# Dividing two query blocks at once, with new ranks and spans in a kernel that schedules itself

## The chip, the cores and the metric

One core of a Trainium2 chip. The metric is the device time of one execution in microseconds (us); most executions agree within 0.3%. A ratio compares with runs of the kernel before on the same chip, in the same rounds. It is the mean time of one kernel's runs over the mean of the other's, so it is not quite the ratio of the medians that stand beside it. The brackets are 95% intervals.

## The reference, cut to what matters

Four layers over a sequence of 2048 rows of 512: attention, FFN, attention, FFN, each on a normalised input and added to the residual. Both attention layers share weights, and so do both FFN layers.

```python
def _A_ref(x, wqkv, wo):                      # 32 heads of 16, window of 256
    ...
    scores = jnp.einsum("bhqd,bhkd->bhqk", q, k) * (Dh ** -0.5)
    mask = (idx[:, None] - idx[None, :] >= 0) & (idx[:, None] - idx[None, :] < W)
    p = _softmax(jnp.where(mask[None, None], scores, -1e9), axis=-1)
    o = jnp.einsum("bhqk,bhkd->bhqd", p, v)
    ...
x = x + _A_ref(_layernorm(x), A_wqkv, A_wo)
x = x + _B_ref(_layernorm(x), B_w1, B_w2)     # 512 -> 1792, relu, -> 512
x = x + _A_ref(_layernorm(x), A_wqkv, A_wo)
x = x + _B_ref(_layernorm(x), B_w1, B_w2)
```

## The kernel before

The sequence is cut into chunks of 512 rows: two attention-and-FFN layers make eight steps k = 0 to 7. The kernel does not issue instructions as its code reads. It first makes a list of operations (each with its possible engines, an assumed duration on each, what it waits for, and a key). Then it plays them through in Python against these assumed durations, and issues each operation when it is chosen there. So the chip gets one fixed order for each engine, and an engine never takes a later instruction because an earlier one still waits. The smallest key goes first on TensorE; the other engines add the key to the time at which an operation became ready.

```python
SOON = {"qkv": 0, "v": 0, "h": 0, "mask": 0, "div": -1, "add": -1}      # ranks of the kinds of work
LINK = {"PE": 0.3, "DVE": 0.2, "ACT": 0.2, "POOL": 0.2, "SP": 0.2}      # assumed delay from one engine to another
...
def choose(e, t):
    ...
        key = (o.key, o.number) if e == "PE" else (at + o.key, o.number)
```

Scores and exponentials have the lowest keys, then P·V (the sums `acc`), the output projection, and last the dense work, which fills the rest. Dense work has its place by number of score group: q, k and v of a step 16 groups ahead of their use, the FFN of a step from d0 to d1 after its last score group.

```python
wait = 0 if k == 0 else 16                                # in plan_qkv: how far ahead q, k, v are made
...
d0, d1 = base[k + 1] + 9, base[k + 1] + 28                # in plan_rest: the span of the FFN
...
t = op(-5, {"SP": (1.22, lambda ...: sp.dma_start_transpose(out=to(), in_=O_of[k][:, j, :]...), 2.6)}, ready, ob, [ob])
```

The last number of the transpose, 2.6, is what the schedule counts from its issue to its landing. When the schedule would leave TensorE idle for 0.4 us or more, it puts in a filler, a matmul of the identity that computes nothing ("warm"):

```python
if t - idle_since[0] >= (0.4 if t > 20 else 0.0) and ...:
    ... mm(box.tile([P, 512], FP32, "warm")[:], ident[:], ...)
```

After P·V of a block of 128 queries (8 heads), VectorE divides by the sums, one block at a time:

```python
def divide(t, j, acc, O, chk):
    rinv = chk[:, j, 8 * t:8 * t + 8].rearrange("p (a e) -> p a e", e=2)
    dve.reciprocal(rinv, acc[:, :, :, 16])
    dve.tensor_tensor(out=O[:, j, P * t:P * (t + 1)]..., in0=acc[:, :, :, 0:16], in1=rinv..., op=ALU.mult)
```

## Time and profile before

| | before |
|---|---|
| time, median of the first 3 runs | 484.17 us (483.27 to 485.19) |
| span of the profiled run | 482.5 us |
| PE, DVE, ACT, POOL busy | 96%, 76%, 70%, 65% |
| granted TensorE clock | 1.00 |

The tables are read with the prediction, which shows their lines. In those lines PE is TensorE, PEld its weight loads, DVE VectorE, ACT ScalarE, POOL GpSimd and SP (SPq) the engine that issues the DMAs. The tiles are: Sps the scores, Pb their exponentials, acc P·V and its sums, chk the inverse sums, O the divided output, OT its transpose by DMA, ps_d a result of dense work, hT the FFN's hidden rows, xn and xnT normalised rows and their transposes, KBD and V2f the spread keys and values, x_sb the residual, ob the output. One number is not in any view and is used all through: the **gaps of TensorE**, the distance of each matmul's start from the start of the one before, less the pitch at which such matmuls follow each other when nothing holds them (the prediction gives the pitches; for the last matmul of a score block it is its usual distance to the next instruction). What is left over is time that TensorE lost, 38.0 us in the kernel before. Some traces lack about 70 matmul records of some 5900; their weight loads are recorded, so the missing places are known, and 216 ns are taken off for each. Time lost to a halved clock is in the gaps, since the pitch is that of the full clock.

### The profile page before, as it was taken

The page shows a single profiled execution, that of the slowest core. Times are in us where ns is not written, and L with a number is a line of the kernel's source. Part 1 is how long each engine was busy: PE and PEld are TensorE (multiplying, and loading weights), DVE is VectorE, ACT ScalarE, POOL GpSimd, SP SyncE. Part 2 cuts the span into 40 slices and gives each one's busy share as a digit, 9 for nine tenths or more (in the row PEclk, how much of TensorE's full clock was granted, in tenths as well). Part 3 has the DMA queues.
Part 4 walks back from the last instruction along what each step waited for, and adds up shares of the span by engine and source line. Part 5 has one row for each costly group of instructions (what it writes and reads, how often), then busy time and mean ns, then how long its engine had stood idle before and what let it go on. Part 6 is the DMA issues. An engine that isn't in the chain of part 4 may idle for free.

```text
span 482.5 us, 14414 instructions
## 1 busy us (share of the span) xinstructions
PE 461.9 (96%) x5935; PEld 242.3 (50%) x5935; DVE 366.4 (76%) x960; ACT 337.2 (70%) x268; POOL 312.4 (65%) x708
## 2 busy tenths in 40 slices
PE   7889899998899999999999999999999999999995
PEld 3555556654445545554544554455555545554442
DVE  6989899858897789878989977898758876473101
ACT  3877877877777767876778877777876787735240
POOL 7778878768876778777878767677655566520000
PEclk9999999999999999999999999999999999999999
DMA  8770231004300142002311023020153002000101
GB/s 271 244 206 3 45 45 25 2 3 67 67 1 3 24 67 46 3 1 45 58 34 33 13 35 47 12 46 1 24 89 57 13 1 56 24 14 12 35 12 37
DMA packets 54649, 21.98 MB, mean 46 GB/s; under 512 B 46128, under 2 KB 54064, under 8 KB 54576
## 3 DMA queue, kind: packets, MB, share of 16 engines
q1 hardware_dynamic: 54576, 20.98, 19.8%
q8 instruction: 48, 0.79, 0.7%
q14 instruction: 25, 0.20, 0.2%
HBM read 7.86 MB, written 2.10 MB: 21 GB/s over the span
## 4 chain that ended last, share of the span: by engine, by line
PE 72%; DVE 10%; DMA 7%; POOL 6%; issue 2%; ACT 2%; DVEq 0%; ACTq 0%; POOLq 0%
PE ps_d L106 52%; PE acc L106 12%; PE Sps L106 8%; DMA OT<-O 4%; POOL Pb L106 3%; ACT Pb L106 2%; DVE KBD L106 1%; DVE st L106 1%; DMA xn2T<-xn 1%; DVE xn L106 1%; DVE Pb L106 1%; POOL xn L106 1%; DVE x_sb L106 1%; DVE V2f L106 1%; DMA xnT<-xn 1%
## 5 line engine op out<-in xcount | busy, mean ns | idle before, releaser
L106 ACT ACTIVATE Pb<-Sps 128x2048 bf16<-128x2048 f32 (+4 forms) x160 | 283.3, 1770 | 94.4 <-PE Sps L106 75.8
L106 POOL TENSOR_SCALAR_AFFINE_SELECT Pb<-Pb 64x256 bf16<-64x256 bf16 x518 | 222.9, 430 | 99.3 <-ACT Pb L106 77.4
L106 PE MATMUL ps_d<-xn2T,w 128*128 128x512 bf16 (+1 forms) x504 | 109.5, 356 | 1.2 <-DVE hT L106 0.9
L106 PE MATMUL ps_d<-w,hT 128*128 128x512 bf16 x448 | 109.0, 380 | 0.0
L106 PEld LDWEIGHTS <-Pb 128*128 128x128 bf16 x2880 | 83.5, 96 | 25.6 <-issue 8.6
L106 PE MATMUL acc<-V2f,Pb 128*128 128x34 bf16 x2880 | 90.1, 178 | 2.3 <-POOL Pb L106 1.3
L106 PE MATMUL ps_d<-xnT,wqkv 128*128 128x512 bf16 (+1 forms) x288 | 66.5, 356 | 2.2 <-DMA xnT<-xn 1.0
L106 PEld LDWEIGHTS <-w 128*128 128x128 bf16 x504 | 45.3, 97 | 44.7 <-issue 5.4
L106 PE MATMUL Sps<-Qt,KBD 32*128 32x192 bf16 (+4 forms) x1472 | 61.6, 252 | 2.8 <-ACT Pb L106 2.5
L106 PEld LDWEIGHTS <-hT 128*128 128x128 bf16 x448 | 40.3, 98 | 46.0 <-issue 3.6
L106 DVE TENSOR_TENSOR Pb<-Pb,tri 128x512 bf16<-128x512 bf16 (+1 forms) x136 | 58.8, 437 | 5.0 <-ACT Pb L106 4.6
L106 DVE TENSOR_SCALAR hT<-ps_d 128x512 bf16<-128x512 f32 (+1 forms) x74 | 45.8, 625 | 11.4 <-PE ps_d L106 10.9
L106 PEld LDWEIGHTS <-KBD 32*128 32x128 bf16 x1472 | 24.0, 92 | 51.7 <-issue 48.9
L106 DVE TENSOR_SCALAR KBD<-ps_d,par 128x256 bf16<-128x256 f32 (+1 forms) x82 | 45.5, 604 | 1.6 <-PE ps_d L106 1.5
L106 DVE BATCH_NORM_STATS2 st<-x_sb 128x6 f32<-128x512 f32 (+1 forms) x64 | 43.7, 683 | 0.9 <-DMA x_sb<-in_A_x_dram 0.6
L106 ACT ACTIVATE hT<-ps_d 128x512 bf16<-128x512 f32 (+1 forms) x52 | 28.4, 550 | 20.9 <-PE ps_d L106 19.4
L106 DVE TENSOR_TENSOR x_sb<-ps_d,x_sb 128x512 f32<-128x512 f32 x48 | 32.7, 684 | 13.0 <-PE ps_d L106 12.4
L106 DVE TENSOR_TENSOR O<-acc,chk 128x128 bf16<-128x128 f32 x128 | 37.3, 291 | 4.5 <-DMA OT<-O 0.2
L106 DVE RECIPROCAL chk<-acc 128x8 f32<-128x8 f32 x128 | 25.6, 200 | 17.7 <-PE acc L106 15.2
L106 PEld LDWEIGHTS <-wqkv 128*128 128x128 bf16 x288 | 25.7, 97 | 26.1 <-issue 4.0
L106 DVE TENSOR_TENSOR ob<-ps_d,x_sb 128x512 bf16<-128x512 f32 x16 | 11.0, 690 | 34.4 <-PE ps_d L106 34.3
L106 PE MATMUL ps_d<-wo,OT 128*128 128x512 bf16 x128 | 32.5, 380 | 3.9 <-DMA OT<-O 3.6
(55 smaller groups left out, 300.3 us busy)
## 6 DMA issues: line engine op xcount, KB each, us to landing
w<-in_B_w_dram SPq DMA_DIRECT2D x2, 1792.0 KB, 10.0
out_dram<-ob SPq DMA_DIRECT2D x16, 128.0 KB, 1.7
wqkv<-in_A_wqkv_dram SPq DMA_DIRECT2D x3, 512.0 KB, 7.0
x_sb<-in_A_x_dram SPq DMA_DIRECT2D x3, 512.0 KB, 8.9
x_sb<-in_A_x_dram SPq DMA_DIRECT2D x2, 256.0 KB, 2.9
wo<-in_A_wo_dram SPq DMA_DIRECT2D x1, 512.0 KB, 8.9
xnT<-xn SPq DMA_TRANSPOSE x28, 2.5
OT<-O SPq DMA_TRANSPOSE x28, 2.5
```

The costliest lines, as they stand in the source:

```text
L106: inst = fn(*a, **k)
```

## The change

The intent: halve the number of divisions, which gives VectorE time back, and set the schedule's ranks and spans anew.

```diff
-    SOON = {"qkv": 0, "v": 0, "h": 0, "mask": 0, "div": -1, "add": -1}
-    LINK = {"PE": 0.3, "DVE": 0.2, "ACT": 0.2, "POOL": 0.2, "SP": 0.2}
+    SOON = {'qkv': -0.5, 'v': 0, 'h': -1, 'mask': -1, 'div': 0, 'add': -2}
+    LINK = {"PE": 0.2, "DVE": 0.2, "ACT": 0.2, "POOL": 0.2, "SP": 0.2}
...
     def divide(t, j, acc, O, chk):
-        rinv = chk[:, j, 8 * t:8 * t + 8].rearrange("p (a e) -> p a e", e=2)
-        dve.reciprocal(rinv, acc[:, :, :, 16])
-        dve.tensor_tensor(out=O[:, j, P * t:P * (t + 1)]..., in0=acc[:, :, :, 0:16], ...)
+        sums = acc[:].rearrange("p j a e d -> p j (a e) d")
+        rinv = chk[:, j:j + 2, 8 * t:8 * t + 8]
+        dve.reciprocal(rinv, sums[:, :, :, 16])
+        dve.tensor_tensor(out=O[:, j:j + 2, P * t:P * (t + 1)]..., in0=sums[:, :, :, 0:16], ...)
...
-            for jl in range(u.nq // 2):
+            for j0 in range(0, u.nq // 2, 2):
                 box = Box(psum)
+                prior = None
+                for jl in (j0, j0 + 1):            # two blocks, one after the other, into one accumulator
...
-                            box.ps = box.tile([P, 4, 2, 17], FP32, "acc")
+                                box.ps = box.tile([P, 2, 4, 2, 17], FP32, "acc")
...
-                divs[k, u.t, j] = op(SOON["div"], {"DVE": (0.5, dfn)}, ...)
+                divs[k, u.t, j] = divs[k, u.t, j + 1] = op(SOON["div"], {"DVE": (0.64, dfn)}, ...)
...
-                d0, d1 = base[k + 1] + 9, base[k + 1] + 28
+                d0, d1 = base[k + 1] + 7, base[k + 1] + 24
```

More of the change, by code (lines that the diff above doesn't have):

```diff
@@ L392, in divide @@
     def divide(t, j, acc, O, chk):
-        rinv = chk[:, j, 8 * t:8 * t + 8].rearrange("p (a e) -> p a e", e=2)
-        dve.reciprocal(rinv, acc[:, :, :, 16])
-        dve.tensor_tensor(out=O[:, j, P * t:P * (t + 1)].rearrange("p (a e d) -> p a e d", a=4, e=2),
-                          in0=acc[:, :, :, 0:16],
-                          in1=rinv.rearrange("p a (e o) -> p a e o", o=1).to_broadcast([P, 4, 2, 16]), op=ALU.mult)
+        sums = acc[:].rearrange("p j a e d -> p j (a e) d")
+        rinv = chk[:, j:j + 2, 8 * t:8 * t + 8]
+        dve.reciprocal(rinv, sums[:, :, :, 16])
+        dve.tensor_tensor(out=O[:, j:j + 2, P * t:P * (t + 1)].rearrange("p j (a d) -> p j a d", d=16),
+                          in0=sums[:, :, :, 0:16],
+                          in1=rinv.rearrange("p j (a o) -> p j a o", o=1).to_broadcast([P, 2, 8, 16]), op=ALU.mult)
     def accumulate_check(chk, first):
@@ L558, in plan_attention @@
                     masks[s].append(op(SOON["mask"], options(times, lambda e, m=m, g=g, pb=pb: mask(e, m, places(pb, g))), [exps[s]] + c_tri))
-            for jl in range(u.nq // 2):
-                kbs = seen(u, jl)
-                need = []
-                for g in sorted({u.place[kb][0] for kb in kbs}):
-                    need += [exps[first_slot[n] + g]] + masks[first_slot[n] + g]
-                for kb in kbs:
-                    b = u.q0 + kb
-                    need.append(v_done[k, b // 2] if b >= 0 else v_done[k - 1, (b + 8) // 2])
-                j = u.q0 // 2 + jl
+            for j0 in range(0, u.nq // 2, 2):
@@ L568, in plan_attention @@
                 box = Box(psum)
                 prior = None
-                for p in range(4):
-                    def pfn(u=u, jl=jl, pb=pb, box=box, p=p):
-                        if p == 0:
-                            box.ps = box.tile([P, 4, 2, 17], FP32, "acc")
-                        pv_group(u, jl, p, pb, box.ps)
-                    prior = op(-5e4 + n - (1000 if p else 0), {"PE": (0.025 * len(kbs) + (0.03 if p == 0 else 0.0), pfn)},
-                               [prior] if p else need, None if p else box, [box])
@@ L578, in plan_attention, with pfn @@
-                pvs[n, jl] = prior
+                for jl in (j0, j0 + 1):
+                    kbs = seen(u, jl)
+                    need = [prior]
+                    for g in sorted({u.place[kb][0] for kb in kbs}):
+                        need += [exps[first_slot[n] + g]] + masks[first_slot[n] + g]
+                    for kb in kbs:
+                        b = u.q0 + kb
+                        need.append(v_done[k, b // 2] if b >= 0 else v_done[k - 1, (b + 8) // 2])
+                    for p in range(4):
+                        begins = jl == j0 and p == 0
+                        def pfn(u=u, jl=jl, j0=j0, pb=pb, box=box, p=p, begins=begins):
+                            if begins:
+                                box.ps = box.tile([P, 2, 4, 2, 17], FP32, "acc")
+                            pv_group(u, jl, p, pb, box.ps[:, jl - j0])
+                        prior = op(-5e4 + n - (0 if begins else 1000),
+                                   {"PE": (0.025 * len(kbs) + (0.03 if p == 0 else 0.0), pfn)},
+                                   need if p == 0 else [prior], box if begins else None, [box])
+                    pvs[n, jl] = prior
@@ L580, in dfn @@
+                j = u.q0 // 2 + j0
                 def dfn(u=u, j=j, box=box):
@@ L583, in plan_attention @@
                 war = [turned[k - 1, i] for i in range(4)] if k else []
-                divs[k, u.t, j] = op(SOON["div"], {"DVE": (0.5, dfn)}, [pvs[n, jl]] + war + checks[k - 2:k - 1], None, [box])
+                divs[k, u.t, j] = divs[k, u.t, j + 1] = op(
+                    SOON["div"], {"DVE": (0.64, dfn)}, [prior] + war + checks[k - 2:k - 1], None, [box])
         checks.append(op(40, {"DVE": (1.1, lambda k=k: accumulate_check(chks[k % 2], k == 0))},
```

## The prediction

> **What bounds the kernel now.** I began with the page's busy shares, went on to the groups of instructions by shape (what one matmul costs), then to the chain of work that ended last in order of time (how fast matmuls follow each other), then to busy time by stretch (where TensorE is idle), and last to the waits.
>
> ```profile
> span 482.5 us, 14414 instructions
> PE 461.9 (96%) x5935; PEld 242.3 (50%) x5935; DVE 366.4 (76%) x960; ACT 337.2 (70%) x268; POOL 312.4 (65%) x708
> ```
>
> ```profile
> 180.86 1.05 PE acc L106 x42
> 184.94 2.27 PE ps_d L106 x10
> 443.10 34.33 PE ps_d L106 x159
> 477.45 0.69 DVE ob L106
> ```
>
> The busy share of PE says little by itself, since a matmul's recorded 380 ns overlaps its neighbours. The pitch in the chain is the true cost: 34.33/159 = 216 ns for a matmul of 512 columns, 1.05/42 = 25 ns for one of the small P·V matmuls (34 columns). The trace starts 256-column matmuls 109 ns and transposes 56 ns apart, and a score group, seen from its start to the start of what follows, takes about 0.33 us. Counts from the groups by shape times these pitches: 1320 x 0.216 = 285.1; 176 x 0.109 = 19.2; 2880 x 0.025 = 72.0; 160 x 0.33 = 52.8; 48 transposes x 0.056 = 2.7; 38 fillers ("warm", which compute nothing) x 0.216 = 8.2. The sum is 440.0 us of the span of 482.5 us. All but the fillers is work that no order of instructions removes.
>
> So 42.5 us are left over. About 1.5 are before the first matmul, and 5.1 after the last one (477.4 us: a last addition on VectorE, then the last store). I took the distance of each start on PE from the one before, less the pitch, over the whole trace: 20.6 us lie in 41 gaps longer than 0.15 us, and 17.4 us in many small ones, above all some 60 ns at each of the 160 entries into a score group. Busy time by stretch shows where PE is plainly idle (columns: length, then busy time of PE, PEld, DVE, ACT, POOL):
>
> ```profile
> 20.00:60.00 40.00, 36.44 (x565) 21.48 (x564) 36.64 (x102) 31.44 (x32) 34.28 (x80) 1.00 0.31 80
> 60.00:105.00 45.00, 43.97 (x656) 26.50 (x653) 38.07 (x108) 34.98 (x26) 33.13 (x75) 1.00 0.13 21
> 105.00:140.00 35.00, 31.25 (x430) 15.78 (x429) 29.84 (x81) 26.62 (x19) 28.69 (x67) 1.00 0.28 47
> 140.00:300.00 160.00, 158.14 (x2184) 80.84 (x2184) 135.78 (x342) 120.53 (x79) 121.48 (x277) 1.00 0.18 30
> 300.00:420.00 120.00, 118.68 (x1620) 61.17 (x1621) 91.62 (x235) 91.66 (x66) 75.27 (x171) 1.00 0.17 34
> ```
>
> The reader is to see that PE is idle 3.6 us in 20 to 60 us and 3.7 us in 105 to 140 us, and only 3.2 us in the 280 us from 140 to 420 us. The granted clock is 1.00 throughout. The waits name VectorE, GpSimd and ScalarE often, but most of these are those engines waiting for work while PE is full:
>
> ```profile
> POOL Pb L106 <- ACT Pb L106: 77.4, 77, 3.9
> ACT Pb L106 <- PE Sps L106: 75.8, 114, 1.7
> DVE chk L106 <- PE acc L106: 15.2, 25, 2.0
> PEld L106 <- DMA OT<-O: 6.7, 9, 1.4
> PE ps_d L106 <- DMA OT<-O: 3.6, 5, 1.2
> ```
>
> **What the Trainium skill says.** "TensorE: Matmul & The Clock Gate", section "Back-to-back issue gap", gives 518 cycles at 2.4 GHz for 512 columns (216 ns) and a floor near 25 ns for up to 64 columns; the trace has exactly these pitches. The same section also names about 131 ns for 512 columns as the sustained figure of a real kernel; this trace, with 216 ns over 159 matmuls, does not agree. "Perfetto Trace Analysis", section "Optimizing Scalar/DVE Operations", says that grouping into larger operations helps if the engine is saturated: VectorE is at 76% of the span, but 85% in 105 to 140 us (29.84 of 35) and 92% in 20 to 60 us. "VectorE: DVE Perf Modes", section on the TRN2 errata, gives (N+151)/0.96 ns for an fp32 addition of two tensors; for the multiplication by the inverse sums it fits this trace: 291 ns at N=128, by the formula 290.6. "PSUM — Partial Sum Buffer", section "The four PSUM rules", says that a bank holds 512 fp32 per partition and that a first matmul clears the accumulation bits of its whole bank: two query blocks are 2 x 136 = 272 fp32 and fit, and the new code closes one block's sums before it opens the next, so nothing is lost. No run here has shown that yet.
>
> **The change part by part.**
>
> ```profile
> L106 DVE TENSOR_TENSOR O<-acc,chk 128x128 bf16<-128x128 f32 x128 | 37.3, 291 | 4.5 <-DMA OT<-O 0.2
> L106 DVE RECIPROCAL chk<-acc 128x8 f32<-128x8 f32 x128 | 25.6, 200 | 17.7 <-PE acc L106 15.2
> ```
>
> 1. The paired division. Removed: 128 x (0.291 + 0.200) = 62.8 us of VectorE. Added: 64 multiplications of 256 elements and 64 reciprocals of 16. Estimates: (256+151)/0.96 = 424 ns; 200 + 8 x 1.04 = 208 ns, the slope from 291 ns at 128 and 684 at 512 elements. 64 x 0.632 = 40.4. Saved: 22.4 us.
>
> 2. What the ranks move between engines. In the order of the built programs VectorE takes 16 more copies into V2f (x 370 ns = 5.9), 4 more double masks (x 495 = 2.0), 2 more normalisations (1.1) and 3 more half evictions of h (1.2), and one less of Q (0.4): +9.8. Net VectorE: 366.4 - 22.4 + 9.8 = about 354 us. GpSimd loses 16 selects (x 430 = 6.9), 16 copies (x 420 = 6.7) and 2 normalisations (2.7): 312 - 16 = 296 us. ScalarE: the same to 1 us.
>
> 3. TensorE. Every count of real matmuls is the same; fillers 40 in place of 38: +0.4 us. Work on PE: 440.0 + 0.4. So none of the saving is on the engine that sets the end, and the change can win only from gaps.
>
> 4. FFN spans and the PE link. The last P·V of the last step stands after 389.0 us of PE work in the order before and after 392.2 us in the new one, so about 3 us of dense work have moved from the tail, where PE is full anyway, into the attention stages. That is worth something only where PE had a gap there. A lower assumed delay of 0.2 in place of 0.3 for PE puts dependants closer behind their producers: fewer planned gaps, more real ones.
>
> 5. The gaps, by what ended them in the trace (of the 20.6 us): DMA of OT 4.5; ScalarE's Pb 4.7; VectorE after the start 4.1; GpSimd's masks 1.9; the rest startup, xnT and the K eviction. From VectorE's I expect half back (-2), from masks and exponentials -1 (mask rank -1, additions -2), from the earlier FFN -1.5. OT I expect to get worse: the division of a pair waits for its second block. In the order the first output projection of a pair stands 3.2 to 4.9 us of PE work behind the last P·V it needs (3.2 in step 1, 3.7 to 3.8 in steps 3 to 5), and in the trace before the projections that stopped PE started 4.4 to 8.0 us after theirs (others were ready after 3.6 to 3.9 us). +1. Sum: -2 - 1 - 1.5 + 1 + 0.4 = -3.1, so 484.2 - 3.1 = about 481 us.
>
> **The rivals.** (a) The saved VectorE time buys nothing, because PE is the bound: for it, 158.14 of 160 us busy from 140 to 300 us. It makes 484. (b) The pair becomes a wait: both transposes of O become ready together, the DMA queue takes them 1.2 us apart, and the residual and norm behind them start later. For it, the OT gaps above; against it, in most steps dense work of the next step stands ready. It makes 486 to 488. (c) The ranks fill the starved stretches: 20 to 60 and 105 to 140 us hold 10.5 us of the gaps over 0.15 us and the 16 fillers outside the start 3.5 us. If most of that went, it would make 474. Against it: the new order has 8 fillers at the first place again, and 12 in place of 8 at the second. (d) The accumulators become scarce: from first to last P·V matmul they are held 146 us in all in place of 84. But there are half as many divisions to wait for, and four buffers x 480 us to be had. It makes no change.
>
> **Range and chances.** Mine lies between (a) and (c), a little nearer to (a). The floor of 432 us of useful matmuls plus start, end and entries leaves about 20 us of gaps, and 2% would be half of them. I predict 481 us, 475.5 to 486.5 eight times in ten. Faster by over 2% (under 474.6): 0.07. Within: 0.89. Slower (over 494): 0.04.
>
> **What would show it.** In the profile after: reciprocals of 128x16 near 208 ns and multiplications of 128x256 near 424 ns, 64 of each; VectorE near 354 us; real matmuls at the same pitches; PE idle less in 105 to 140 us; waits of PE and PEld for OT as large as before or larger. If VectorE falls and PE's gaps do not, (a) is right. If the starved stretches vanish and the time is under 475 us, I have sized the ranks too small; if PE waits for OT grow by several us, (b) is right.

## The result, and the profile after

482.47 us median (481.79 to 482.80, 4 runs) against 484.23 us (483.27 to 485.19, 4 runs). The ratio is 0.9962 [0.9939, 0.9985]: a gain of 0.4%, inside the 2% that count as the same. In later rounds, on chip 14 (kernel 5 below), the two kernels could not be told apart.

The page after, first two lines; beside the lines before, VectorE has 104 instructions and 6.7 us less, GpSimd 11.7 us less. (PE lacks 73 of its 5937 records here, as the count beside PEld shows, so its busy time is too small.)

```profile
span 479.9 us, 14186 instructions
PE 454.9 (95%) x5864; PEld 242.1 (50%) x5937; DVE 359.7 (75%) x856; ACT 337.1 (70%) x266; POOL 300.7 (63%) x670
```

The groups by shape of the division after (busy, mean ns of one, idle before):

```profile
L106 DVE TENSOR_TENSOR O<-acc,chk 128x256 bf16<-128x256 f32 x64 | 27.1, 424 | 2.5 <-DVE chk L106 0.3
L106 DVE RECIPROCAL chk<-acc 128x16 f32<-128x16 f32 x64 | 16.1, 252 | 17.1 <-PE acc L106 16.5
```

The division took 37.3 + 25.6 = 62.9 us before and takes 27.1 + 16.1 = 43.2 us now: 19.7 us are saved.

Waits after (total us, times, longest), for the lines shown of before:

```profile
POOL Pb L106 <- ACT Pb L106: 89.0, 86, 4.4
ACT Pb L106 <- PE Sps L106: 73.4, 113, 2.3
DVE chk L106 <- PE acc L106: 16.5, 29, 2.1
PEld L106 <- DMA OT<-O: 9.9, 16, 1.9
PE ps_d L106 <- DMA OT<-O: 3.9, 4, 1.5
```

Waits of TensorE and its weight loads for the transposed O have grown from 6.7 + 3.6 to 9.9 + 3.9 us, in 20 places in place of 14. One of them, in the chain in order of time: the transpose takes 4.19 us from its issue until the output projection can start, where the schedule counts 2.6.

```profile
112.53 0.44 DVE O L106
112.97 0.11 SPq L106
113.07 0.04 issue
113.12 4.19 DMA OT<-O
117.31 0.05 issue
117.35 1.91 PE ps_d L106 x8
```

The gaps of TensorE by stretch, all sizes:

| stretch, us | before | after |
|---|---|---|
| 0 to 20 | 5.1 | 5.4 |
| 20 to 60 | 7.1 | 5.5 |
| 60 to 105 | 3.1 | 2.5 |
| 105 to 140 | 6.2 | 5.1 |
| 140 to 300 | 9.8 | 10.7 |
| 300 to 420 | 6.4 | 5.2 |
| after 420 | 0.1 | 0.0 |
| sum | 38.0 | 34.2 |

So 3.8 us of gaps went, two more fillers cost 0.4, and the last addition on VectorE starts at 474.10 us in the chain after where it started at 477.45 us before: 3.35 us earlier. The last store took some 0.7 us longer in this profile, so the span is 2.6 us shorter; the medians differ by 1.8 us.

### The profile page after: what moved, and what is told of

Same layout as the page of the kernel before. It is cut to its first block, busy times and chain, and to the rows that moved or that the text cites. A ratio compares the mean times of both kernels' runs of the same rounds, so it can differ in the third digit from the quotient of the medians.

```text
span 479.9 us, 14186 instructions
## 1 busy us (share of the span) xinstructions
PE 454.9 (95%) x5864; PEld 242.1 (50%) x5937; DVE 359.7 (75%) x856; ACT 337.1 (70%) x266; POOL 300.7 (63%) x670
## 4 chain that ended last, share of the span: by engine, by line
PE 72%; POOL 8%; DMA 7%; DVE 6%; issue 3%; ACT 2%; POOLq 0%; DVEq 0%; ACTq 0%; SPq 0%
PE ps_d L106 51%; PE acc L106 13%; PE Sps L106 8%; POOL Pb L106 4%; DMA OT<-O 3%; DMA xnT<-xn 3%; ACT Pb L106 2%; POOL xn L106 2%; POOL V2f L106 1%; DVE st L106 1%; POOL rstds L106 1%; DVE V2f L106 1%; DVE KBD L106 1%; DVE xn L106 1%; POOL nbs L106 1%
## 5 line engine op out<-in xcount | busy, mean ns | idle before, releaser
L106 POOL TENSOR_SCALAR_AFFINE_SELECT Pb<-Pb 64x256 bf16<-64x256 bf16 x502 | 219.9, 438 | 109.6 <-ACT Pb L106 89.0
L106 PE MATMUL ps_d<-xn2T,w 128*128 128x512 bf16 (+1 forms) x486 | 106.8, 355 | 2.4 <-issue 0.9
L106 PE MATMUL ps_d<-w,hT 128*128 128x512 bf16 x427 | 103.7, 379 | 1.7 <-issue 1.0
L106 PEld LDWEIGHTS <-Pb 128*128 128x128 bf16 x2880 | 83.5, 96 | 25.6 <-issue 9.3
L106 DVE TENSOR_TENSOR Pb<-Pb,tri 128x512 bf16<-128x512 bf16 (+1 forms) x140 | 61.5, 444 | 16.9 <-ACT Pb L106 16.5
L106 PE MATMUL ps_d<-xnT,wqkv 128*128 128x512 bf16 (+1 forms) x271 | 63.7, 354 | 2.9 <-issue 1.1
L106 PE MATMUL Sps<-Qt,KBD 32*128 32x192 bf16 (+4 forms) x1472 | 61.5, 252 | 1.0 <-ACT Pb L106 0.7
L106 DVE TENSOR_SCALAR hT<-ps_d 128x512 bf16<-128x512 f32 (+1 forms) x77 | 46.6, 617 | 12.4 <-PE ps_d L106 12.3
L106 ACT ACTIVATE hT<-ps_d 128x512 bf16<-128x512 f32 (+1 forms) x49 | 27.5, 561 | 22.4 <-PE ps_d L106 22.0
L106 POOL TENSOR_TENSOR rstds<-rstds,mhalf 128x2 f32<-128x2 f32 (+1 forms) x33 | 23.6, 718 | 14.5 <-DVE rstds L106 12.0
L106 PE MATMUL ps_d<-wqkv,xnT 128*128 128x512 bf16 x118 | 31.4, 379 | 0.6 <-issue 0.2
```

The source lines that it names most:

```text
L106: inst = fn(*a, **k)
```

## The experiments

Twelve kernels ran, four at a time on one chip each, all with five rounds and all with the reference's results. The table gathers them. "Account" is the time that the kernel's own scheduler comes to by its assumed durations; "lost" is fillers x 0.216 us plus the gaps, both of the profiled run.

| kernel | fillers | gaps, us | of these over 0.15 us and ended by OT | lost, us | account, us | median, us | ratio to before |
|---|---|---|---|---|---|---|---|
| before (profile of its first runs) | 38 | 38.0 | 4.5 | 46.2 | 482.2 | 484.2 | |
| changed | 40 | 34.2 | 5.5 | 42.8 | 480.3 | 482.47 | 0.9962 [0.9939, 0.9985] |
| 1 pair alone | 44 | 37.0 | 3.7 | 46.5 | 483.3 | 485.08 | 1.0016 [1.0002, 1.0031] |
| 2 ranks alone | 34 | 42.3 | 6.3 | 49.6 | 484.9 | 486.50 | 1.0033 [1.0019, 1.0048] |
| 3 spans alone | 38 | 38.2 | 3.9 | 46.4 | 483.9 | 484.78 | 1.0007 [0.9994, 1.0020] |
| 4 changed, VectorE padded | 40 | 37.6 | 5.2 | 46.2 | 480.3 | 485.09 | 1.0027 [1.0007, 1.0047] |
| 5 changed, again | 40 | 34.7 | 4.9 | 43.3 | 480.3 | 483.53 | 1.0005 [0.9982, 1.0028] |
| 6 changed, span end 23 | 53 | 35.2 | 5.4 | 46.6 | 483.7 | 485.49 | 1.0046 [1.0019, 1.0072] |
| 7 single, searched | 36 | 35.6 | 3.6 | 43.4 | 478.7 | 481.89 | 0.9972 [0.9948, 0.9995] |
| 8 changed without the pair | 34 | 45.0 | 6.7 | 52.3 | 483.7 | 487.77 | 1.0090 [1.0064, 1.0117] |
| 9 pair, 3.2 us, searched | 34 | 31.1 | 1.0 | 38.5 | 477.3 | 477.60 | 0.9867 [0.9845, 0.9890] |
| 10 single, 3.2 us, searched | 36 | 30.7 | 2.2 | 38.5 | 479.4 | 477.09 | 0.9864 [0.9844, 0.9884] |
| 11 as 9, searched, no fillers | 20 | 34.2 | 1.0 | 38.5 | 477.1 | 479.59 | 0.9910 [0.9894, 0.9926] |
| 12 as 10, searched, no fillers | 20 | 37.8 | 1.0 | 42.1 | 478.8 | 481.02 | 0.9938 [0.9923, 0.9953] |

Kernels 1 to 4 shared 11 runs of before with a median of 484.56 us, 5 to 8 a median of 483.74, 9 to 12 a median of 484.08. Each kernel has 4 to 6 runs. In kernels 11 and 12 one wait of 1.4 us lies between two score blocks that follow each other directly; it is counted here.

Two things in this table are to be kept in mind. First, gaps and lost are those of one run. The profiled runs of kernels 1, 2 and 8 are slower than their medians (486.19, 487.94 and 490.48 us), and in each of them the granted clock is halved for 3.4 us in mid-kernel (6.8 us in kernel 8). By the gaps within these windows that took 1.1, 1.5 and 2.6 us. Second, the account needs no chip. Kernel 5 repeats the changed kernel, and the account doesn't see the padding of kernel 4; for the other eleven, whether the account lies above or below that of the kernel before agrees with whether the median does. The sizes do not: kernel 10 was 2.8 us shorter by the account and 7.0 us on the chip.

**First set: which part made the gain?** I held that the ranks had made it (theory A); the rivals were the freed VectorE time (B) and the FFN spans (C).

Kernel 1, the pair alone:

```diff
 (the paired division of the change)
+    SOON = {"qkv": 0, "v": 0, "h": 0, "mask": 0, "div": -1, "add": -1}     # as before
+    LINK = {"PE": 0.3, ...}                                                # as before
+                d0, d1 = base[k + 1] + 9, base[k + 1] + 28                 # as before
```

> The kernel before with the paired division alone; old ranks, old PE link, old FFN spans. Theory A (the ranks made the gain; the pair only frees VectorE, which is not the bound, and delays the output projections): 484 to 485.5 us, with VectorE some 20 us less busy than before, 44 fillers in the order in place of 38, and larger waits for OT. Rival B (the freed VectorE time made the gain): about 482 us, gaps that VectorE ends gone.

Measured: 485.08 us, ratio 1.0016. VectorE was 353.9 us busy, 12.5 less than before where I expected 20, and the order has 44 fillers. The forecast of A holds for the time, not in its reason: the gaps ended by OT did not grow (3.7 us). The gaps fell by 1.0 us (the profiled run's half-clock window, 1.1 us, included) and the six fillers more cost 1.3. VectorE time was freed here, and what it may have bought went into fillers.

Kernel 2, the ranks and the link alone:

```diff
+    SOON = {'qkv': -0.5, 'v': 0, 'h': -1, 'mask': -1, 'div': 0, 'add': -2}
+    LINK = {"PE": 0.2, ...}
```

> The kernel before with the new ranks and the PE link of 0.2 alone; single divisions, old spans. Theory A: about 482 us or a little below, with fewer gaps between 20 and 60 us and after 300 us; its order has 34 fillers in place of 38. Rival B: 484 us, as before. Rival C (the FFN spans made the gain): 484 us.

Measured: 486.50 us, ratio 1.0033, slower than before. Theory A falls. The order has the fewest fillers of this set but the most gaps, 42.3 us, of which 1.5 lie in a half-clock window. The scheduler's own account, 484.9 us against 482.2, had said slower too.

Kernel 3, the spans alone:

```diff
-                d0, d1 = base[k + 1] + 9, base[k + 1] + 28
+                d0, d1 = base[k + 1] + 7, base[k + 1] + 24
```

> The kernel before with the new FFN spans alone (7 to 24 in place of 9 to 28). The order is the same up to about the 70th score group. Theory A: 484 us within 1 us, because PE is already full after 140 us. Rival C: about 482 us, with the gaps after 300 us gone.

Measured: 484.78 us, ratio 1.0007. C falls too. After 300 us the gaps went from 6.4 to 4.9 us, but between 140 and 300 us they rose from 9.8 to 12.0. The gaps were moved and not removed.

So no part gains by itself: +0.16, +0.33 and +0.07%, and yet all three together gained 0.4% in the first rounds. The parts don't add. (By the account they don't either: 483.3, 484.9 and 483.9 us for the parts, 482.2 for the kernel before, 480.3 for the whole.)

Kernel 4, the changed kernel's own order with VectorE made slower by an instruction that does nothing:

```diff
         dve.tensor_tensor(out=O[:, j:j + 2, ...], in0=sums[:, :, :, 0:16], ...)
+        dve.tensor_tensor(out=tri[:], in0=tri[:], in1=tri[:], op=ALU.min)
```

> The changed kernel with one idle VectorE instruction (a minimum of a constant with itself, some 0.25 to 0.3 us) after each of the 64 paired divisions; order and scheduler's times unchanged. It gives back 16 to 19 us of the 19.7 us of VectorE time that the pairing freed. Theory A: 482.5 to 483.2 us, at most 0.7 us slower than the changed kernel. Rival B: 484 us or more, the gain gone.

The instructions on this tile in the profile of kernel 4 (ns min/median/max, first and last start):

```profile
L106 DVE TENSOR_TENSOR tri<-tri x64: 246/250/470, 22.9 to 429.9; 128x192 bf16<-128x192 bf16 x64
```

Measured: 485.09 us, ratio 1.0027. 64 x 0.25 = 16 us of VectorE time brought the gaps from 34.2 back to 37.6 us, 1.8 us of it between 20 and 60 us. Against the kernel before nothing of the changed kernel's gain is left. The changed kernel did not run in these rounds, though; its ratios elsewhere, 0.9962 and 1.0005 (kernel 5), put the cost of the padding at 0.7% or 0.2%, 1 to 3 us. So in a fixed order VectorE's time does seem to count, by some 2 us for 16: this speaks for B, where kernel 1 speaks against it. The two differ in one thing. In kernel 4 the order stays, and in kernel 1 the scheduler made a new order out of the shorter divisions.

**Second set: is it the order?** A new theory (D): each alteration of a number gives another order, orders differ by some us whatever the reason for the alteration, and the settings of the change are ones that came out well with the pair. The rival (E): pair and ranks belong together, and their gain is robust.

Kernel 5 is the changed kernel, unaltered.

> The changed kernel once more, as the base of this set: 482 to 483 us, 0.4% under the kernel before, if the first result holds on this chip.

Measured: 483.53 us beside 483.74 for the kernel before, ratio 1.0005 [0.9982, 1.0028]. The profile agrees with the first one (gaps 34.7 us, span 480.5), but three of the six runs had a mean granted clock of 0.994 to 0.995 and took 484.0 to 484.3 us; the other three took 482.3 to 483.1. No run of the kernel before had under 0.998 here. The third set comes back to this.

Kernel 6, one number altered by one:

```diff
-                d0, d1 = base[k + 1] + 7, base[k + 1] + 24
+                d0, d1 = base[k + 1] + 7, base[k + 1] + 23
```

> The changed kernel with one number altered by one: the FFN span ends at 23 in place of 24. Pair and ranks stay. Theory D (the gain is that of one particular instruction order out of many; every small alteration of a rank gives another order, and the new settings are a picked one): the scheduler's own account lengthens by 3.4 us and the order has 53 fillers in place of 40, so 484.5 to 487 us, slower than the kernel before. Theory E (the gain belongs to the paired division together with the ranks and is robust): within 1 us of the changed kernel.

Measured: 485.49 us, ratio 1.0046, that is 0.4% over the changed kernel in the same rounds. Busy time of the fillers alone, by stretch, between 140 and 300 us, first in the changed kernel, then in kernel 6:

```profile
140.00:300.00 160.00, 0.00 (x0) 1.00 0.16 30
```

```profile
140.00:300.00 160.00, 3.15 (x13) 1.00 0.15 28
```

The gaps hardly differ (35.2 to 34.7 us). 13 fillers, 2.8 us at their pitch, stand where the changed kernel has real work: by the schedule the FFN has run out there. A step of one group in one span costs more than the whole change brought. E falls.

Kernel 7, single divisions with other numbers. The scheduler can be run without a chip in a fraction of a second, so I let a random search alter ranks, spans and lead some 4000 times. I took the settings with the best mean of two accounts, with 2.6 and with 3.3 us for a transpose; the order itself is made with 2.6, as before:

```diff
-    SOON = {"qkv": 0, "v": 0, "h": 0, "mask": 0, "div": -1, "add": -1}
-    LINK = {"PE": 0.3, "DVE": 0.2, "ACT": 0.2, "POOL": 0.2, "SP": 0.2}
+    SOON = {'qkv': 0.5, 'v': 0.25, 'h': -1.5, 'mask': 2, 'div': -3, 'add': -3}
+    LINK = {"PE": 0.2, "DVE": 0.2, "ACT": 0.2, "POOL": 0.2, "SP": 0.2}
-        wait = 0 if k == 0 else 16
+        wait = 0 if k == 0 else 17
-                d0, d1 = base[k + 1] + 9, base[k + 1] + 28
+                d0, d1 = base[k + 1] + 15, base[k + 1] + 31
```

> The kernel before with single divisions, and ranks and spans that I searched for with the scheduler's own account (q, k, v 0.5, v 0.25, h -1.5, mask 2, div -3, add -3; span 15 to 31; qkv lead 17; PE link 0.2). Theory D: single divisions do as well as the pair when the order is picked for them: the account says 1.7 us less than the changed kernel, so 480 to 482.5 us. Theory E (the freed VectorE time is needed): 484 us or more.

Measured: 481.89 us, ratio 0.9972 [0.9948, 0.9995]. With single divisions, and VectorE 362.7 us busy, it does as well as the changed kernel: 0.9972 beside 0.9962 in the first rounds and 1.0005 in these. D holds.

Kernel 8, the changed kernel with its division undone and all its settings kept:

```diff
 (the division of before)
+    SOON, LINK, d0 and d1 of the change
```

> The changed kernel with its division undone: new ranks, link and spans, single divisions. Theory D: these settings were picked with the pair, so without it the order is an arbitrary one: 484 to 486.5 us (the scheduler's account is 3.4 us above that of the changed kernel). Theory E says the same, so it tells only whether the pair is needed with these very settings. If the pair were worthless in them, 482.5 us.

Measured: 487.77 us, ratio 1.0090, a little more than I expected. (Its profiled run spent 6.8 us at half clock, from 187.2 us on.) With kernel 5 this makes the pair look worth 0.9%; with kernel 1 it looks worth -0.2%; with kernel 7, nothing. A part that is undone here takes the order with it, so such a comparison measures two orders and not the part.

**Third set: can the order be chosen for what the chip does?** In nearly all of the traces so far the output projections that stop TensorE wait for a transpose for which the schedule counts 2.6 us. The instructions on OT in the changed kernel's profile show what it takes:

```profile
DMA to landing us min/median/max: 2.4/2.5/4.2
```

The median is right; the tail is not: 8 of the 28 took more than 2.6 us. A fixed order that counts on the median stops whenever the transpose comes late. Kernels 9 to 12 count 3.2 us for every transpose of O and of the normalised rows, and have ranks, spans and lead searched anew under that count, each for its own division (some 1900 trials each).

```diff
-                    out=to(), in_=O_of[k][:, j, :].rearrange(...)), 2.6)}, ready, ob, [ob])
+                    out=to(), in_=O_of[k][:, j, :].rearrange(...)), 3.2)}, ready, ob, [ob])
-        return op(0, {"SP": (1.22, dma, 2.6)}, [a], None, [box])
+        return op(0, {"SP": (1.22, dma, 3.2)}, [a], None, [box])
 kernel 9, paired:
+    SOON = {'qkv': 0, 'v': 1, 'h': -1, 'mask': 0.5, 'div': 0.25, 'add': -3}     # lead 24, span 15 to 28
 kernel 10, single:
+    SOON = {'qkv': 0.5, 'v': 1, 'h': -3, 'mask': -2, 'div': -3, 'add': -3}      # lead 8, span 12 to 35
```

> Paired division; the scheduler counts 3.2 us in place of 2.6 from a transpose's issue to its landing (the traces showed it too short), and ranks, spans and the qkv lead (24) are searched for anew under that count. Its account is 477.3 us, its order has 34 fillers. Theory D (the chosen order decides, and the pair widens the choice by some VectorE time): 478 to 481 us, faster than both kernels, with the gaps that OT ends under 3 us. If the account is not to be trusted at this level: 482 to 485 us.

> The same with single divisions: 3.2 us for a transpose, own searched ranks, spans and lead; account 479.4 us, 36 fillers. Theory D: 480 to 483 us, 0.3 to 0.5% behind the paired one of this set, which is then what the 20 us of freed VectorE time are worth when each has its own order. If the pair is worth nothing: the same time as the paired one within 0.5 us.

Measured: 477.60 us for the pair (ratio 0.9867) and 477.09 us for single divisions (0.9864). Both beat both kernels, by more than I expected, and they don't differ. The waits for OT, first of kernel 9, then of kernel 10:

```profile
PEld L106 <- DMA OT<-O: 1.2, 2, 0.7
PE ps_d L106 <- DMA OT<-O: 0.6, 1, 0.6
```

```profile
PEld L106 <- DMA OT<-O: 2.8, 4, 1.8
PE ps_d L106 <- DMA OT<-O: 2.1, 2, 1.6
```

And kernel 10's busy time by stretch (PE, PEld, DVE, ACT, POOL), to be held against the same stretches of the kernel before in the prediction:

```profile
20.00:60.00 40.00, 38.11 (x592) 23.37 (x594) 37.64 (x103) 33.62 (x33) 32.12 (x74) 1.00 0.34 85
105.00:140.00 35.00, 32.07 (x494) 17.15 (x493) 31.01 (x84) 27.60 (x20) 27.41 (x61) 1.00 0.31 47
140.00:300.00 160.00, 159.93 (x2193) 81.85 (x2192) 133.58 (x340) 123.68 (x85) 118.28 (x264) 1.00 0.17 32
300.00:420.00 120.00, 119.71 (x1575) 60.78 (x1574) 91.03 (x237) 93.12 (x69) 73.74 (x164) 1.00 0.16 33
```

TensorE is busy 159.93 of 160 us in the long middle, where it was 158.14, and 38.11 of 40 in the early stretch, where it was 36.44. VectorE in kernel 10 is as loaded as before: 364.4 us in all, against 349.8 in kernel 9. The scheduler's account had put the pair 2.1 us ahead; the chip does not show it. The two searches found different places (leads of 24 and of 8 groups), so this compares the best orders found and not every possible one.

Where the gaps went is not only where the prediction saw TensorE idle. In the two stretches of 20 to 60 and 105 to 140 us they fell by 3.2 us in kernel 9 and in kernel 10 alike; between 140 and 420 us, where TensorE's busy share is 99% in the kernel before, they fell from 16.2 to 13.7 and 12.4 us. A busy share hides such gaps, because a matmul's record (380 ns) is longer than its pitch (216 ns).

Kernels 11 and 12 leave the fillers out after the start:

```diff
-                if t - idle_since[0] >= (0.4 if t > 20 else 0.0) and ...:
+                if t - idle_since[0] >= (99.0 if t > 20 else 0.0) and ...:
 kernel 11, paired:  SOON = {'qkv': -0.5, 'v': 1, 'h': -0.25, 'mask': -0.5, 'div': 0.25, 'add': -2}   # lead 23, span 2 to 23
 kernel 12, single:  SOON = {'qkv': 0, 'v': 1, 'h': -1.5, 'mask': 0, 'div': -1.5, 'add': -2}          # lead 12, span 10 to 28
```

> The paired division, 3.2 us for a transpose, searched anew, and no fillers after the start (20 in place of 34). Account 477.1 us. If fillers only cost their PE time where real work could have come: as the paired one with fillers, 478 to 481 us. If they are needed to keep TensorE's granted clock: a lower granted clock in the records and 2 us or more longer.

> Single divisions, 3.2 us for a transpose, searched anew, no fillers after the start. Account 478.8 us. Theory D: 480 to 482.5 us, behind its paired counterpart by 0.3 to 0.5%, as the account says (1.7 us).

Measured: 479.59 and 481.02 us, 2.0 and 3.9 us behind their counterparts with fillers, although by the account they should have been 0.1 and 0.6 us ahead. The granted clock tells a part of why. It averaged 0.991 to 0.992 in all six runs of kernel 12 and 0.988 to 0.995 in the four of kernel 11, against 0.994 to 0.999 with fillers. (Their ranks differ too, so the records of the clock carry this more than the times do. And a mean also counts the end of a run: in all profiles but kernel 7's the last 0.1 to 3.7 us, after the last matmul, are at half clock and cost nothing. Kernel 9's mean of 0.996 is that alone.) Kernel 12 by stretch, with the granted clock as the third number from the end:

```profile
47.50:51.00 3.50, 1.12 (x36) 0.89 (x36) 2.90 (x8) 3.00 (x3) 3.14 (x8) 0.98 0.35 68
51.00:54.30 3.30, 3.30 (x57) 2.26 (x54) 1.87 (x7) 1.37 (x1) 2.88 (x8) 0.50 0.15 28
```

In the 3.5 us up to 51 us TensorE worked 1.12 us; then it had half its clock for the next 3.4 us, with work at hand. Page "TensorE: Matmul & The Clock Gate", section "What's actually happening", tells of an activity monitor that halves the clock after an idle window of 3413 ns. The trace agrees with the half and with the length (the records give 3413 ns), but the window need not be idle: here 32% of it was busy. In kernel 12's profile there are two such windows, which by the gaps within them took 1.8 of the 3.6 us that it lost more than kernel 10 (42.1 to 38.5). Kernel 11's profiled run is its fastest, with one window (1.2 us), and lost no more than kernel 9's. Kernel 2 shows the same once, around a wait for OT:

```profile
313.00:316.60 3.60, 1.84 (x62) 1.57 (x62) 3.43 (x12) 3.47 (x3) 2.84 (x8) 1.00 0.27 52
316.60:320.00 3.40, 3.09 (x8) 1.17 (x9) 1.99 (x7) 0.78 (x1) 1.93 (x5) 0.50 0.35 68
```

There 51% was busy. The half-clock records in mid-kernel last 3.41 us, or twice that in kernel 8. With this as a grid over the fourteen profiles, from 7 us to the last matmul, half clock followed all four windows that were busy for less than 36%, two of the five between 46% and 56%, and none above, but that in kernel 8 it stayed for a second window. Such a window costs up to half its length, 1.7 us, which is as much as the whole change brought; by the gaps within them they took 0.7 to 1.5 us each. The slow half of kernel 5's runs had a mean clock lower by 0.003, about one such window (3.4 us x 0.5 / 483 = 0.0035), and were 1.4 us slower. None of those runs is the profiled one, and up to 0.004 of a mean can be the end of the run, so that it was such a window is argued, not shown.

## Why the prediction was right or wrong

The time held: 481 forecast, 482.47 measured, the same within 2%. Of the reasons, some held.

- **PE is the bound.** Held. Pitches and counts are the same, fillers 40 as counted, and the span of a profile less "lost" lies between 436.1 and 437.9 us in all fourteen of them: what an order costs is its gaps and its fillers. The prediction's own parts do not close, though: 440.0 + 1.5 + 5.1 + 38.0 is 484.6 us, and the span 482.5. Its 0.33 us for a score group holds waits that are counted as gaps once more; without them it is 0.316 us, 2.3 us less in all. And an entry into a score group costs 95 ns in the median, not 60: entries are 13.8 of the 17.4 us of small gaps.
- **The division** (step 1). The multiplication took 424 ns, as the formula said. The reciprocal took 252 ns where I had 208: I gave it the slope of the multiplication (1.04 ns per element), and it has 6.5 ns per element (from 200 to 252 ns over 8 more). Saved: 19.7 us, not 22.4.
- **What moves between engines** (step 2). VectorE came to 359.7 us, not 354. Besides the reciprocals, the masks on VectorE grew from 58.8 to 61.5 us where I had counted 2.0 us more (the small ones from 340 to 375 ns each), and the copies into V2f by 6.5 where I had 5.9. GpSimd came to 300.7 us, not 296: its selects took 438 ns each in place of 430.
- **The gaps** (step 5). The sum came out as forecast, -3.8 + 0.4 where I had -3.5 + 0.4. Of those over 0.15 us, the ones that OT ends rose from 4.5 to 5.5 us, as forecast. VectorE's, apart from the start, fell from 4.1 to 1.3 (forecast: 2 off). Those of masks and exponentials fell by 2.8 (6.6 to 3.8), not by 1, all of it from the exponentials. That the sum fits is in part luck: what the exponentials brought too much stands in for the FFN's term. And the gaps of the two profiles fell by 3.8 us where the medians fell by 1.8, and by nothing that could be told on chip 14.
- **The FFN spans** (step 4). I had given them 1.5 us. Alone they moved gaps from after 300 us to before it and won nothing, and in the changed kernel, too, what went after 300 us (6.4 to 5.2) came back between 140 and 300 us (9.8 to 10.7). I see nothing of this term; how much the spans give together with the new ranks, no run shows.
- **Rival (a), saved VectorE time buys nothing.** Wrong as a general sentence: with the order fixed, 16 us of VectorE time cost some 2 us (kernel 4, 1 to 3 by the ratios). Right in effect once the order is made anew (kernels 1, 9 and 10).
- **Rival (b), the pair becomes a wait.** Its mechanism was seen, at its small size: 1 us.
- **Rival (c), the ranks fill the starved stretches.** They did not by themselves (kernel 2). But 477 us was nearer than I thought: kernels 9 and 10 reached it with 7 us of gaps less, 3.2 of them from those stretches and 2.5 to 3.8 from 140 to 420 us.
- **Rival (d), the accumulators become scarce.** No run tests it alone. VectorE's gaps fell, so nothing of it is seen.
- **The step that failed** is the sum itself. I added a term for each part, as if each had a worth of its own. Kernels 1, 2, 3 and 8 show that they have none apart from the order that they make together. The rival that I did not name is that any alteration makes another order, which has to be priced as a whole: kernel 6 lost 0.4% by one step in one number, and kernel 7 won 0.3% without the pair. It is not a mere draw. The scheduler's account, which I could have run before I predicted, was 1.9 us shorter for the change and longer for each of its parts.

The gain of the change itself remains small and not certain: 0.4% in the first rounds; on chip 14 the ratio was 1.0005 [0.9982, 1.0028]. What I could not settle is how much of the 1.35% of kernels 9 and 10 comes from the count of 3.2 us and how much from the search that came with it. Kernel 7 had a search too, but its order is made with the old count; it won only 0.3%, which speaks for the count, and so does the fall of the OT gaps; but a search can also be lucky.

## What to carry to other kernels

In a kernel whose static order comes from a scheduler, undoing one part makes another order, so a comparison of parts measures orders; hold the order fixed and pad one engine when the question is what that engine's time is worth, with the unpadded kernel in the same rounds. Ask the scheduler's own account of the whole order before adding up parts. Before tuning ranks, hold the scheduler's assumed durations against the trace, tails included: a transfer that is counted at its median stops an in-order engine each time it is late. Keep the engine that bounds the kernel fed even with empty work where a stretch is thin, if the granted clock shows that it is halved after such a stretch; here the kernels without fillers, which had other ranks too, were 2.0 and 3.9 us slower.

## What the Trainium skill lacked or had wrong

- "TensorE: Matmul & The Clock Gate", section "What's actually happening": the half clock is put down to an idle window (the section "A second HAM failure mode: psum-queue depth-cycling" also tells of frequent short idles, without a share). Here windows in which TensorE was busy 32% and 51% of the time (1.12 of 3.5 us, 1.84 of 3.6 us) were followed by 3.4 us at half clock, and one that was busy 47% (kernel 10, before 115.8 us) was not.
- The same page, section "Back-to-back issue gap": the sustained 131 ns for 512 columns in real kernels did not appear; 159 matmuls in a row took 216 ns each.
- No page that I found has the duration of VectorE's reciprocal on small tiles from PSUM: 200 ns for 128x8, 252 ns for 128x16.
- "DMA: Bandwidth & Descriptors" has no time from issue to landing for a transpose of 128x512 bf16 within SBUF: in the changed kernel 2.4 us at least and 2.5 in the median; 4.2 at most for O, and 4.5 for the normalised rows.
- No page that I found says that a trace can lack matmul records: 73 of 5937 in the changed kernel's, none in the kernel before's.
